# Seven block products in place of eight in one layer of a mixture-of-experts kernel, with its sums on VectorE and its row scatters respaced

## The chip, the core and the metric

The kernel runs on one core of a Trainium2 chip. TensorE (PE) multiplies, VectorE (DVE) and ScalarE (ACT) read its results from PSUM and work on SBUF, GpSimd (POOL) issues the indirect DMAs that scatter rows, and SyncE (SP) issues the other DMAs. [...]The metric is the device time of one execution in microseconds. Three runs of the kernel before took 1376.5, 1378.32 and 1379.24 us; the median is 1378.32.

## The reference

Two parts follow each other. The first takes the real part of a two-dimensional Fourier transform of each of 8 batches of 2496 rows and 256 columns. The second is a mixture of experts without dropped rows: each of the 19,968 rows goes to the one expert of eight that its logits choose, through two layers, and is scaled with its gate's probability.

```python
X = np.fft.fft(x, axis=1)
X = np.fft.fft(X, axis=2)
x = X.real.astype(np.float32).reshape(B * S, D)
...
logits = x @ w_gate
expert_idx = np.argmax(logits, axis=1)
...
for e in range(E):
    lo, hi = (boundaries[e], boundaries[e + 1])
    h = np.maximum(x_sorted[lo:hi] @ w1[e], 0.0)
    y_sorted[lo:hi] = h @ w2[e]
return (gate_w[:, None] * y).astype(np.float32)
```

Here D is 256, the hidden width F is 1024, and everything is float32.

## The kernel before

The work has two streams that are woven into one program by Python generators. The order of all instructions is written out by hand: each `yield` is a place where the other stream may put in its next piece.

**The side stream** makes rows out of a batch. `first` (L314) loads x, folds it on VectorE (L284 to L286, L295) and multiplies (tile s); its result passes through DRAM (`Td`, read back by `regroup`). `second` (L350) finishes the transform with the products p2 and p3 (both named p in the profile), copies on ScalarE (zz L368, zs L394, the mirrored rows L373) and the row sums on VectorE (lg L397, rows L399). `route` (L405) picks each row's expert and its place, ranks rows with small matmuls (rk), and scatters ten groups of 128 rows with indirect DMAs into the sorted store `Xs` in DRAM, one per yield. A batch is done in two halves, so it has 20 scatters. `close` then runs `plan` (L456), a chain of small VectorE instructions that turns the counts into a table of blocks: which rows of `Xs`, and which expert.

**The main stream** is `experts` (L530). It goes through 66 blocks in eight rounds; round b uses what batches 0 to b have put into `Xs`. Rounds 0 and 1 have blocks of 256 and 128 rows, round 2 has three blocks of 512 rows, rounds 3 to 7 have five of 512 rows each, and round 7 ends with 7 blocks of 256 and up to 21 of 128 rows. `fetch` (L504) loads a block's rows xb and its expert's w1 and w2 on SP's queue, one or two blocks ahead, three buffers each. `turn` (L517) transposes the rows of the next block on TensorE (tile pt) and VectorE writes them to xT. The first layer of a 512-row block has 8 chunks of 128 hidden columns; each chunk is a PSUM bank ph with two matmuls (the halves of D), and a Relu takes it to hT, by ScalarE (L584) for even chunks and VectorE (L582) for odd ones. The second layer has four output tiles py of 128 rows with eight matmuls each; ScalarE scales them into y (L598) and GpSimd scatters them to the output (L222). The transposes of the next block stand ahead of the first and second output tile.

**The weaving.** While round b-1 is worked on, batch b passes through `second` and batch b+1 through `first`; `mixed` (L632) is that side stream. Every chunk of the first layer counts one unit of work and every output tile two, 16 units a 512-row block. The main loop gives the side stream 44 ticks over 70% of a round's units:

```python
due += TICKS * w / (0.7 * total) if w else 1
while due >= 1:
    next(side, None)
    due -= 1
```

[...]three (`pm_`) for the side stream, two for ph, two for py and one for pt. All matmuls are recorded at L207 and all indirect DMAs at L222, since helpers issue them; they are told apart by their tiles.

Of the kernel before, what the change touches and what calls it, by code (L numbers as in the profile page):

```python
# [11 lines left out]
F32 = mybir.dt.float32  # L12
BF16 = mybir.dt.bfloat16
I32 = mybir.dt.int32
ALU = mybir.AluOpType
ACTF = mybir.ActivationFunctionType
AX_X = mybir.AxisListType.X
PSUM = bass.MemoryType.PSUM
# [162 lines left out]

TICKS = 44
WARM = 16
MOST = max(k for now in rounds() for _, k, _ in now)


# [15 lines left out]
def kernel(ctx: ExitStack, tc, x, w_gate, w1, w2, out):  # L202
# [39 lines left out]
    pm_ = ctx.enter_context(tc.tile_pool(name="pm_", bufs=3, space=PSUM))  # L242
    pst = ctx.enter_context(tc.tile_pool(name="pst", bufs=1, space=PSUM))
    psh = ctx.enter_context(tc.tile_pool(name="psh", bufs=2, space=PSUM))
    psy = ctx.enter_context(tc.tile_pool(name="psy", bufs=2, space=PSUM))

# [158 lines left out]
    def route(b, h, rows, lg):  # L405
# [40 lines left out]
        for s in range(NSL):  # L446
            sent(put_row(Xs, pi[:, s:s + 1], rows[:, s], E * CAP - 1, "xs"), b)
            yield

# [66 lines left out]

    def turn(size, xb):  # L517

        xT = bp.tile([128, 2, BIG], F32, tag="xT", name="xT", bufs=1)
        n = min(size // 128, 2)  # L520
        for h in range(-(-size // 256)):
            pt = pst.tile([128, 2, n, 128], F32, tag="t", name="pt")
            for c in range(2):
                for t in range(n):
                    nc.tensor.transpose(pt[:, c, t], xb[:, 2 * h + t, c * 128:(c + 1) * 128], ident[:])  # L525
            vec.tensor_scalar(xT[:, :, 256 * h:256 * h + 128 * n], pt[:].rearrange("p c t k -> p c (t k)"),  # L526
                              con["alt"][:], None, op0=ALU.mult)
            yield xT

    def experts(todo):  # L530

        got, xT, used = [], None, None

# [20 lines left out]
        for k, (b, size, last, at) in enumerate(todo):  # L556
            n, m = size // 128, BIG // size
            if not k:
                while todo[0][:3] not in tabs:
                    yield 0  # L560
                fetch_some(0)
                for _ in range(9):
                    yield 0
                for xT in turn(size, got[0][0]):
                    pass
# [6 lines left out]
            hT = bp.tile([128, FC, BIG], F32, tag="hT", name="hT", bufs=1)  # L572
            for f in range(FC // m):
                ph = psh.tile([128, m, size], F32, tag="h", name="ph")
                with needed(last, at, ph):
                    for j in range(m):
                        for c in range(2):
                            mm(ph[:, j], w1_sb[:, c, (m * f + j) * 128:(m * f + j + 1) * 128], xT[:, c, 0:size],
                               c == 0, c == 1)
                o = hT[:, m * f:m * (f + 1), 0:size]  # L580
                if f % 2:
                    vec.tensor_scalar(o, ph[:], 0.0, None, op0=ALU.max)  # L582
                else:
                    act.activation(o, ph[:], ACTF.Relu)  # L584
                yield 1
            if follow:
                while follow[:3] not in tabs:
                    yield 0
                fetch_some(k + 1, 2)
                turned = turn(follow[1], got[0][0])  # L590
            y = bp.tile([128, BIG // 128, D], F32, tag="y", name="y", bufs=3)
            for i in range(n):
                xT = next(turned, xT)
                py = psy.tile([128, D], F32, tag="y", name="py")
                with needed(last, at, py):
                    for f in range(FC):
                        mm(py[:], hT[:, f, i * 128:(i + 1) * 128], w2_sb[:, f], f == 0, f == FC - 1)
                act.activation(y[:, i], py[:], ACTF.Copy, scale=xb[:, i, D + 1:D + 2])  # L598
                put_row(out, ro[:, i:i + 1], y[:, i], NT - 1, "out")
                yield 2  # L600
            for xT in turned:
                pass

    def pads(b):
# [27 lines left out]
    def mixed(b):  # L632
# [5 lines left out]
        for k, _ in enumerate(two):  # L638
            if k % 2:
                next(one, None)  # L640
            yield
        yield from woven(close(b), one)

# [8 lines left out]
    nc.sync.dma_start(out=wg[:], in_=w_gate)  # L652
    for _ in range(WARM):
        pw = psy.tile([128, D], F32, tag="y", name="py")
        mm(pw[:], ones[:], bc(ones[:], 1, 2))
# [30 lines left out]
    for k, _ in enumerate(second(0)):  # L686
        if k % 2 == 0:
            next(early, None)
    work = experts(todo)
    for b in range(1, B):  # L690

        side, done, due = mixed(b), 0, 0.0
        if b == 1:
            side = woven(close(0), chain(early, side))
        total = 16 * sum(k * size for size, k, _ in rounds()[b - 1]) / BIG
        while done < total:
            w = next(work)
            done += w
            due += TICKS * w / (0.7 * total) if w else 1
            while due >= 1:  # L700
                next(side, None)
                due -= 1
        for _ in side:
            pass
    rest = pads(B - 1)
# [51 lines left out]
```

## Time and profile before

| | |
|---|---|
| median of three runs | 1378.32 us |
| profiled execution, its own time | 1381.33 us |
| span of its instructions | 1379.6 us |
| granted TensorE clock, mean over the span | 0.975 |
| ph, first layer (2016 matmuls, all block sizes) | 577.8 us busy |
| py, second layer (2560 matmuls) | 572.0 us busy |
| output scatters (163) on GpSimd | 159.1 us busy |
| row scatters (160) on GpSimd | 158.7 us busy |

A line of the groups reads: line, engine, operation, output tile, input tiles, shapes, count; then busy time and the mean length of one in ns; then the engine's idle time ahead of them and what ended most of it. A line of a timeline reads: start and length in us, engine, line, operation, tiles, count, and in brackets the idle time before it. The granted clock is below 1 in the first quarter of the span only: 0.73 from 0 to 100 us, 0.97 from 100 to 350 us, and 1.00 after that.

### The profile page before, as it was taken

The page shows a single profiled execution, that of the slowest core. Times are in us where ns is not written, and L with a number is a line of the kernel's source. Part 1 is how long each engine was busy: PE and PEld are TensorE (multiplying, and loading weights), DVE is VectorE, ACT ScalarE, POOL GpSimd, SP SyncE. Part 2 cuts the span into 40 slices and gives each one's busy share as a digit, 9 for nine tenths or more (in the row PEclk, how much of TensorE's full clock was granted, in tenths as well). Part 3 has the DMA queues.
Part 4 walks back from the last instruction along what each step waited for, and adds up shares of the span by engine and source line. Part 5 has one row for each costly group of instructions (what it writes and reads, how often), then busy time and mean ns, then how long its engine had stood idle before and what let it go on. Part 6 is the DMA issues. An engine that isn't in the chain of part 4 may idle for free.

```text
span 1379.6 us, 16917 instructions
## 1 busy us (share of the span) xinstructions
PE 1317.9 (96%) x6055; PEld 992.2 (72%) x6055; DVE 380.7 (28%) x1183; ACT 282.7 (20%) x656; POOL 325.8 (24%) x335
## 2 busy tenths in 40 slices
PE   5688898999999999999999999999999999999998
PEld 3567787676677677776677667776666779999887
DVE  4552244333232213332232221333211111111111
ACT  1322032221132112221132211221111111111111
POOL 0334224033122311324113311224131111111111
PEclk6779999999999999999999999999999999999999
DMA  8768756652555242553424342232452226777785
GB/s 252 244 240 297 284 191 218 260 177 83 234 177 177 82 176 103 192 184 129 157 85 139 142 174 92 107 119 78 162 190 93 88 87 240 264 273 273 257 316 199
DMA packets 63089, 249.50 MB, mean 181 GB/s; under 512 B 10057, under 2 KB 24883, under 8 KB 43420
## 3 DMA queue, kind: packets, MB, share of 16 engines
q1 hardware_dynamic: 46231, 203.33, 41.6%
q0 software_dynamic: 15888, 42.14, 8.4%
q10 hardware_dynamic: 885, 2.94, 0.6%
q8 instruction: 49, 0.80, 0.2%
q14 instruction: 36, 0.29, 0.1%
HBM read 194.97 MB, written 54.83 MB: 181 GB/s over the span
## 4 chain that ended last, share of the span: by engine, by line
PE 88%; issue 4%; DMA 3%; DVE 2%; another core or an unknown queue 1%; POOL 1%; ACT 1%; SPq 0%; POOLq 0%; ACTq 0%; DVEq 0%
PE py L207 39%; PE ph L207 38%; PE p L207 5%; PE s L207 3%; PE pt L525 3%; DMA xq<-in_x_dram 2%; POOL Xs L222 1%; DMA out_dram<-y,ro 1%; DMA Td<-t 0%; DVE hT L582 0%; DMA t<-Td 0%; DVE xq L295 0%; PE rk L207 0%; DMA xb<-Xs 0%
## 5 line engine op out<-in xcount | busy, mean ns | idle before, releaser
L207 PE MATMUL ph<-xT,w_sb 128*128 128x512 f32 (+2 forms) x2016 | 577.8, 440 | 11.2 <-ACT hT L584 2.6
L207 PE MATMUL py<-w_sb,hT 128*128 128x256 f32 x2560 | 572.0, 380 | 6.1 <-issue 6.1
L207 PEld LDWEIGHTS py<-w_sb,hT 128*128 128x128 f32 x2560 | 479.4, 190 | 67.8 <-issue 6.5
L207 PEld LDWEIGHTS ph<-xT,w_sb 128*128 128x128 f32 x2016 | 328.2, 192 | 209.8 <-issue 175.7
L222 POOL DMA_INDIRECT out_dram<-y,ro x163 | 159.1, 976 | 871.2 <-ACT y L598 848.4
L582 DVE TENSOR_SCALAR hT<-ph 128x512 f32<-128x512 f32 x163 | 112.7, 692 | 695.9 <-issue 330.6
L598 ACT ACTIVATE y<-py,xb 128x256 f32<-128x256 f32 x163 | 77.3, 474 | 606.0 <-PE py L207 525.4
L222 POOL DMA_INDIRECT Xs<-rows,pi x160 | 158.7, 992 | 177.0 <-issue 79.5
L584 ACT ACTIVATE hT<-ph 128x512 f32<-128x512 f32 x163 | 97.3, 597 | 320.7 <-PE ph L207 281.1
L526 DVE TENSOR_SCALAR xT<-pt,table 128x512 f32<-128x512 f32 (+1 forms) x94 | 63.4, 674 | 64.0 <-PE pt L525 62.5
L207 PE MATMUL s<-xq,w 104*112 104x256 f32 (+2 forms) x208 | 62.7, 426 | 12.2 <-DVE xq L286 11.1
L207 PEld LDWEIGHTS p<-table,t 120*128 120x128 f32 x352 | 55.0, 205 | 26.1 <-issue 19.4
L207 PE MATMUL p<-table,zz 128*128 128x145 f32 (+1 forms) x320 | 58.2, 308 | 9.3 <-ACT zz L368 4.6
L207 PE MATMUL p<-table,t 120*128 120x120 f32 (+1 forms) x352 | 58.2, 291 | 8.4 <-issue 5.2
L397 DVE COPY lg<-p 128x16 f32<-128x16 f32 x80 | 13.9, 174 | 189.4 <-ACT zs L394 164.5
L207 PEld LDWEIGHTS s<-xq,w 104*112 104x112 f32 x208 | 39.9, 207 | 25.8 <-DVE xq L286 9.8
L207 PEld LDWEIGHTS p<-table,zz 128*128 128x128 f32 x320 | 46.8, 199 | 14.2 <-issue 7.0
L525 PEld LDWEIGHTS pt<-table,xb 128*128 128x128 f32 x326 | 40.5, 142 | 17.6 <-issue 12.9
L525 PE MATMUL pt<-table,xb 128*128 128x128 f32 x326 | 51.7, 274 | 0.4 <-DMA xb<-Xs 0.4
L399 DVE SCALAR_TENSOR_TENSOR rows<-p,zs 128x129 f32<-128x129 f32 x160 | 48.3, 344 | 1.6 <-issue 0.6
L368 ACT COPY zz<-p 128x240 f32<-128x240 f32 (+1 forms) x88 | 31.1, 353 | 46.5 <-PE p L207 37.0
L310 ACT COPY t<-s 112x512 f32<-112x512 f32 x48 | 28.0, 584 | 54.8 <-PE s L207 44.6
(83 smaller groups left out, 305.6 us busy)
## 6 DMA issues: line engine op xcount, KB each, us to landing
w_sb<-in_moe_w_dram SPq DMA_DIRECT2D x132, 1024.0 KB
xq<-in_x_dram SPq DMA_DIRECT2D x24, 896.0 KB
xb<-Xs SPq DMA_DIRECT2D x28, 516.0 KB
Td<-t SPq DMA_DIRECT2D x18, 448.0 KB
t<-Td SPq DMA_DIRECT2D x8, 768.0 KB
t<-Td SPq DMA_DIRECT2D x8, 640.0 KB
xb<-Xs SPq DMA_DIRECT2D x13, 258.0 KB
xb<-Xs SPq DMA_DIRECT2D x25, 129.0 KB
```

The costliest lines, as they stand in the source:

```text
L207: nc.tensor.matmul(o, lhsT=lhsT, rhs=rhs, start=start, stop=stop, **kw)
L222: return unordered(pool.indirect_dma_start(out=dst, out_offset=bass.IndirectOffsetOnAxis(ap=idx, axis=0), in_=rows, in_offset=None, bounds ...
L310: act.copy(t1[:, 2 * half:2 * half + 2], ps[:])
L368: act.copy(zz[:, :, g * GP:g * GP + n], p2[:])
L397: vec.tensor_copy(lg[:, k:k + 2], p3[:, NY:NY + 2 * E].rearrange("p (m e) -> p m e", m=2))
L399: vec.scalar_tensor_tensor(rows[:, k + m, 0:NY], p3[:, 0:NY], zs[:, 0:1], zs[:, 1:], op0=ALU.add, op1=op)
L525: nc.tensor.transpose(pt[:, c, t], xb[:, 2 * h + t, c * 128:(c + 1) * 128], ident[:])
L526: vec.tensor_scalar(xT[:, :, 256 * h:256 * h + 128 * n], pt[:].rearrange("p c t k -> p c (t k)"), con["alt"][:], None, op0=ALU.mult)
L582: vec.tensor_scalar(o, ph[:], 0.0, None, op0=ALU.max)
L584: act.activation(o, ph[:], ACTF.Relu)
L598: act.activation(y[:, i], py[:], ACTF.Copy, scale=xb[:, i, D + 1:D + 2])
```

## The change

In rounds 3 to 7 the first layer of each 512-row block, the product of rows (512 x 256) with w1 (256 x 1024), is cut into two by two by two blocks and made from seven block products in place of eight, in Winograd's form of Strassen's scheme.

- `turn` adds, at its end, four differences of the halves of xT on VectorE (256 columns each, `right`).
- `Left` makes four sums and differences of quarters of w1 (512 columns each, two written over or beside w1 in `ws`). They are issued one at a time by `step`, two in each group of the preceding block's first layer.
- `seven` takes the place of the loop over chunks: two groups, each with seven products of 2 chunks x 256 rows in five PSUM banks a to e. Two products add onto a bank that still holds another (a and c). ScalarE copies the first product (p1), VectorE forms u2, u3 and three hidden quarters from PSUM, ScalarE applies the Relu.
- PSUM: the two ph, two py and one pt banks become the five banks a to e; blocks of the old kind use a and c for ph, b and d for py, e for pt.
- The output tile y becomes a tile for each 128 rows, with six buffers.
- A group of row scatters is put on a list (`waiting`), and `send` issues one: with every tick before batch 4; from batch 4 on, one for each 1.2 units of work, also within `seven`.
- No side work is woven into `seven` (its yields are marked full). The side stream gets 32 ticks over 65% of the units outside `seven`; the second layer's tiles of these blocks yield twice, with one unit each.

```diff
-TICKS = 44
+TICKS = 32
+LATE = 4
+SHARE, ROOM = 0.65, 1.2
+def halved(b, size):
+    return size == 512 and b > 2
...
         for s in range(NSL):
-            sent(put_row(Xs, pi[:, s:s + 1], rows[:, s], E * CAP - 1, "xs"), b)
-            yield
+            waiting.append((b, pi[:, s:s + 1], rows[:, s]))
...
+    class Left:
+        def __init__(self, w1_sb):
+            ws = bp.tile([128, 3, F // 2], F32, tag="ws", name="ws", bufs=2)
+            o = [ws[:, k] for k in range(3)]
+            a11, a12, a21, a22 = (w1_sb[:, c, k * F // 2:(k + 1) * F // 2] for k in range(2) for c in range(2))
+            self.all = a11, a12, o[2], a22, o[0], o[1], a21
+            self.due = deque([(o[0], a21, a22, add), (o[1], o[0], a11, sub), (a21, a11, a21, sub),
+                              (o[2], a12, o[1], sub)])
...
+    def right(xs, b11, b12, b21, b22):
+        o = [xs[:, k] for k in range(3)]
+        vec.tensor_tensor(o[0], b12, b11, op=sub)
+        vec.tensor_tensor(o[1], b22, o[0], op=sub)
+        vec.tensor_tensor(b12, b22, b12, op=sub)
+        vec.tensor_tensor(o[2], b21, o[1], op=sub)
+        return b11, b21, b22, o[2], o[0], o[1], b12
...
+        def product(g, k, o, fresh=True):
+            for j in range(fp):
+                f = g * fp + j
+                mm(o[:, j], l[k][:, f * 128:(f + 1) * 128], r[k], fresh and not j, j == fp - 1, skip_group_check=True)
+        for g in range(half // fp):
+            a, b, c, d, e = (pse.tile([128, fp, th], F32, tag=k, name=k) for k in "abcde")
...
+            product(g, 0, a)
+            act.copy(p1[:], a[:])
+            yield
+            product(g, 5, b)
+            vec.tensor_tensor(u2[:], p1[:], b[:], op=add)
+            yield
+            product(g, 6, d)
+            vec.tensor_tensor(u3[:], u2[:], d[:], op=add)
+            yield
+            product(g, 4, c)
+            vec.tensor_tensor(h22, u3[:], c[:], op=add)
+            step()
+            yield
+            product(g, 1, a, False)
+            act.activation(h11, a[:], ACTF.Relu)
+            act.activation(h22, h22, ACTF.Relu)
+            yield
+            product(g, 3, e)
+            vec.tensor_tensor(h21, u3[:], e[:], op=add)
+            act.activation(h21, h21, ACTF.Relu)
+            yield
+            product(g, 2, c, False)
+            vec.tensor_tensor(h12, u2[:], c[:], op=add)
+            act.activation(h12, h12, ACTF.Relu)
+            step()
+            yield
...
+            more = None
+            if follow and got and halved(follow[0], follow[1]):
+                more = Left(got[0][1])
+            if halved(b, size):
+                for _ in seven(size, left.all, xT, hT, more.step if more else lambda: None):
+                    yield 0.5, True
...
-                y = bp.tile([128, BIG // 128, D], F32, tag="y", name="y", bufs=3)
+                y = bp.tile([128, D], F32, tag="y", name="y", bufs=6)
...
-        total = 16 * sum(k * size for size, k, _ in rounds()[b - 1]) / BIG
+        blocks = [(size, k * size / BIG, halved(b - 1, size)) for size, k, _ in rounds()[b - 1]]
+        total = sum(k * (15 if seven_ else 16) for _, k, seven_ in blocks)
+        open_ = sum(k * (8 if seven_ else 16) for _, k, seven_ in blocks)
         while done < total:
-            w = next(work)
+            w, full = next(work)
             done += w
-            due += TICKS * w / (0.7 * total) if w else 1
+            if not full:
+                due += TICKS * w / (SHARE * open_) if w else 1
             while due >= 1:
                 next(side, None)
                 due -= 1
+                if b < LATE or not w:
+                    send()
+            room = min(room + w, 2)
+            if b >= LATE and room >= ROOM:
+                send()
+                room -= ROOM
```

## The prediction

> **What bounds the kernel now.** I read the page first: shares of engines, then the chain that ended last.
>
> ```profile
> PE 1317.9 (96%) x6055; PEld 992.2 (72%) x6055; DVE 380.7 (28%) x1183; ACT 282.7 (20%) x656; POOL 325.8 (24%) x335
> ...
> PE 88%; issue 4%; DMA 3%; DVE 2%; another core or an unknown queue 1%; POOL 1%; ACT 1%; SPq 0%; POOLq 0%; ACTq 0%; DVEq 0%
> ```
>
> TensorE is busy for 96% of the span and holds 88% of the chain. Busy matmuls overlap (one lasts 380 ns, the next starts sooner), so I measure them by spacing. The timeline of PE alone, over one 512-row block of round 4 without side work and the start of the next, gives it:
>
> ```profile
> 653.47 13.90 PE L207 MATMUL ph<-xT,w_sb 128*128 128x512 f32 x32
> 667.20 0.60 PE L525 MATMUL pt<-table,xb 128*128 128x128 f32 x4
> 667.64 3.62 PE L207 MATMUL py<-w_sb,hT 128*128 128x256 f32 x16
> 671.09 0.60 PE L525 MATMUL pt<-table,xb 128*128 128x128 f32 x4
> 671.53 10.53 PE L207 MATMUL py<-w_sb,hT 128*128 128x256 f32 x48
> 681.89 10.46 PE L207 MATMUL ph<-xT,w_sb 128*128 128x512 f32 x24
> ```
>
> The reader sees two things. First, the code issues 16 first-layer matmuls for a block (8 chunks times 2 halves of D) and the trace has 32: **each f32 matmul runs as two**. Missing this halves the gain and makes VectorE look like the bound. Second, there are no holes. The spacing is (13.90-0.59)/31 = 0.429 us for 512 columns, with 0.59 the last one's own length, and (10.53-0.38)/47 = 0.216 us for 256 columns: nearly the same per column. The granted clock is 1.00 from 350 us on, and the table by stretches shows PE busy for 771.1 of the 775 us from 350 to 1125. So time taken off PE here comes off the span, if nothing else fills it.
>
> The groups by shape give the other durations:
>
> ```profile
> L582 DVE TENSOR_SCALAR hT<-ph 128x512 f32<-128x512 f32 x163 | 112.7, 692 | 695.9 <-issue 330.6 <-PE ph L207 303.1 <-remote 34.0
> L584 ACT ACTIVATE hT<-ph 128x512 f32<-128x512 f32 x163 | 97.3, 597 | 320.7 <-PE ph L207 281.1 <-issue 34.1 <-remote 4.0
> L399 DVE SCALAR_TENSOR_TENSOR rows<-p,zs 128x129 f32<-128x129 f32 x160 | 48.3, 344 | 1.6 <-issue 0.6
> L284 DVE TENSOR_TENSOR xq<-xq 104x508 f32<-104x508 f32 x24 | 16.3, 681 | 0.3
> L284 DVE TENSOR_TENSOR pm<-xq 104x127 f32<-104x127 f32 x8 | 2.3, 284 | 12.0 <-DMA xq<-in_x_dram 12.0
> ```
>
> **Products removed.** Rounds 3 to 7 have five 512-row blocks each, 25 in all. Before, a block's first layer is 32 x 0.429 = 13.74 us. After, it is 7 products x 4 chunks x 2 = 56 matmuls of 256 columns: 56 x 0.216 = 12.10 us. Gain 1.64 us a block, **41.1 us** in all. The doubled weight loads (190 ns each) stay under the 0.216 us spacing, as in the py stretch.
>
> **Sums added.** VectorE gets 10 sums from PSUM, 4 weight sums (512 wide) and 4 row sums (256 wide) a block and loses 4 evictions; ScalarE has 10 instructions for 4. A weight sum is the 508-column row, 0.68 us. A row sum lies between the rows of 127 and 508 columns: 0.42 us. A sum of PSUM and SBUF has no row of its width: from below 0.68 us (SBUF alone); L399 reads PSUM and takes 344 ns for 129 columns where L284 takes 284 for 127, so I add 0.06: 0.75 us. VectorE gains 7.5+2.7+1.7-2.8 = 9.1 us a block, 228 us in all, on an engine now at 28%. The question is whether the order makes PE wait.
>
> In the stage only products stand on PE; side work waits for the second layer. One product is 4 matmuls, 0.864 us, and its result is there 0.65+0.38 = 1.03 us after its start. ScalarE takes 0.60; a handover is 0.04 in the trace. First group, from the start of the stage: p1 copied 1.07-1.67; u2 waits for the second product, 1.93-2.68; u3 2.80-3.55; h22 3.66-4.41; weight sum to 5.0; h21 5.39-6.14; the seventh product wants c at 5.18 and h22 has read it by 4.41; h12 6.25-7.00, its Relu to 7.64. Second group from 6.05: its p1 copy stands behind that Relu on ScalarE, 7.64-8.24; u2 8.28-9.03, u3 9.07-9.82, h22 9.86-10.61 (needed at 11.23); h21 waits for its product, 11.44-12.19. The next transposes use bank e, which h21 reads: they start at 12.23, PE was ready at 12.10. So PE waits 0.13 us a block: **+3.3 us**. Behind them py reads its last hidden chunks only after six pairs of matmuls; they are there.
>
> Each of these needs has 0.6 to 0.8 us to spare, so a VectorE or ScalarE that enters late costs little. Some 12 stages follow second layers full of side work; a lag of 1.5 us would push h22 past 5.18 by 0.66: at most +8 us, at least 0; I take **+2**, since the last side evictions (0.27+0.17+0.60 us) end about when u2 starts.
>
> Row sums are issued at the third output tile and first needed two tiles (6.9 us) later; left sums a stage ahead. That adds a wait on the next block's w1 in VectorE's queue, in front of h21. In round 4 the plan ended at 645.3 and its loads were issued from 646.6, inside a second layer that ended at 653.5; after, the plan again stands in the fourth block's second layer, some 11 us before the first left sum. Cost 0.
>
> **Scatters against VectorE.** [...]The trace of the opening shows both orders:
>
> ```profile
> 65.52 1.21 DVE L295 TENSOR_TENSOR xq<-xq 104x1024 f32<-104x1024 f32 x1
> ...
> 65.80 1.78 POOL L222 DMA_INDIRECT Xs<-rows,pi  x1 [0.30 <-issue]
> ...
> 75.70 0.97 POOL L222 DMA_INDIRECT Xs<-rows,pi  x1 [0.30 <-issue]
> 75.79 0.68 DVE L284 TENSOR_TENSOR xq<-xq 104x508 f32<-104x508 f32 x1
> ```
>
> A scatter that starts under a sum is longer by 0.8; a sum that starts under a scatter keeps its 0.68. [...]By the row: 0 for VectorE, up to 0.7 us a scatter for GpSimd (24% busy). I take the row: 0.
>
> **Side work.** Its PE work is unchanged and stands in the second layers, about 1.2 ticks per 1.73 us of py. Before, a tick came per 2.2 us, but eight of 14 py turns in a round had two in a row; after, some six of 26 turns have two. Cost 0; rival 1 prices the rest. The block plan leaves the first layer, where its chain of small VectorE instructions held up an hT eviction:
>
> ```profile
> 636.95 1.98 PE L207 MATMUL ph<-xT,w_sb 128*128 128x512 f32 x4 [0.94 <-DVE p_nb L466]
> ```
>
> The windows at 470, 630, 790 and 940-960 us show PE idle for 3.8 us in all. In the second layer only the row transposes hang on VectorE, with 3.4 us to spare: **-3.8** (ends -3.8 and 0). Rounds 0 to 2 change only in pace and scatters. POOL sends batch 0 back to back (1.28 us apart) from 52.9 to 80.5, and still will. PE idles 19 us from 100 to 350; I put ±6 on that, taken as 0. Output tiles: six single tiles for three of four rows hold 20 us of work against a write of some 7 us; banks a to e give every other block the two buffers it had, but for py of 128-row blocks, which has a 3.6 us ph stage between two uses and a 0.47 us eviction: 0.
>
> **Sum.** -41.1+3.3+2-3.8 = -39.6. The profiled execution took 1381.3 (span 1379.6): 1341.7. It lies 3.0 above the median of the runs, 1378.3, so a median of **1339**.
>
> **Rivals.**
> 1. Side work, squeezed into the second layers, makes PE wait for the small evictions between ticks. For it: the double tick at 706.33 took 2.99 us where its matmuls fill 2.74, so 0.25 was lost. Against: that stretch is 100% busy elsewhere. If half of 35 ticks in each of four rounds lose 0.25: +17, 1356; if all: 1374. Chance 0.13.
> 2. VectorE bounds the stage. If a sum from PSUM and SBUF ran at two cycles per element (the 1.22 us of the 1024-column L295), nine sums, three weight sums and the copies before the last h21 take 1.9+9x1.26+3x0.64+0.6 = 15.8 us against 13.74: +2.0 a block where the forecast has -1.5, 50.5 in all, less the 3.8 of the plan: 1425, **slower**. It decides from about 0.99 us a sum. Against: pos<-rk,base from PSUM and SBUF (215 ns, 80 columns) is no longer than pos<-pos,oh from SBUF alone (246). Chance 0.06.
> 3. The stage fits but its gain is lost elsewhere (late w1 at round changes, a longer opening): within 0.2% of before. Chance 0.02.
>
> The forecast has 0.79, between 1326 (no wait for e, opening -6) and 1355 (all lags, opening +6). To leave out no more than 0.2, the range runs to 1358. About 0.2% is what a measurement tells from no change. Faster 0.92, same 0.02, slower 0.06.
>
> **What will show it.** 56 matmuls of 256 columns in a stage at 0.216 us; stages of 12.1 to 12.4 us between P0 and the transposes, and a pt wait of about 0.1 us on h21; sums from PSUM at 0.69 to 0.75 us; VectorE near 610 us busy; the PE gaps at the plan gone. It is wrong if PE idles over 1 us in a stage, or between ticks of the second layer.

## The result, and the profile after

| | before | after |
|---|---|---|
| median of four runs each, the first pair | 1377.41 us | 1364.72 us |
| ratio, 95% interval | | 0.991 [0.989, 0.993] |
| profiled execution, span | 1379.6 us | 1362.3 us |
| start of the first 512-row block of round 3 | 360.8 us | 367.4 us |
| its 25 blocks of rounds 3 to 7 | 778.1 us | 753.9 us |

The change makes the kernel faster, but by 13 us at the medians and 17 us between the profiled spans, where the forecast had 39.6. The last two rows, taken from TensorE's timelines, say where: the opening loses 6.6 us, and the 25 blocks gain 24.2.

The page of the kernel after, shares of engines and the chain:

```profile
PE 1284.0 (94%) x6655; PEld 1103.7 (81%) x6655; DVE 581.0 (43%) x1533; ACT 368.9 (27%) x806; POOL 326.1 (24%) x335
...
PE 87%; DVE 4%; DMA 3%; issue 3%; another core or an unknown queue 1%; ACT 1%; POOL 0%; SPq 0%; POOLq 0%; DVEq 0%; ACTq 0%
```

VectorE is 200 us busier and still at 43%. New in the chain are VectorE's 4% (2 before). The timeline of TensorE over a block of round 4 without side work and without row scatters in its stage:

```profile
652.05 1.03 PE L215 MATMUL a<-xT,w_sb 128*128 128x256 f32 x4
652.91 1.03 PE L215 MATMUL b<-xs,ws 128*128 128x256 f32 x4
...
663.27 1.03 PE L215 MATMUL c<-xT,ws 128*128 128x256 f32 x4
664.22 0.66 PE L567 MATMUL pt<-table,xb 128*128 128x128 f32 x4
...
678.97 1.03 PE L215 MATMUL a<-xT,w_sb 128*128 128x256 f32 x4
```

A product comes every 0.863 us, the stage from the first product to the transposes is 12.17 us, and the block 26.92, where the same block was 28.43 before (653.47 to 681.89): 1.51 less, as the forecast had it. The loss is in other stages. The groups by shape:

```profile
L215 PE MATMUL a<-xT,w_sb 128*128 128x256 f32 x400 | 103.3, 381 | 5.0 <-ACT p L597 4.3 <-issue 0.8
L567 PE MATMUL pt<-table,xb 128*128 128x128 f32 x326 | 53.3, 279 | 10.8 <-DMA xb<-Xs 9.9 <-DVE hT L614 0.4
L215 PE MATMUL c<-xT,ws 128*128 128x256 f32 x200 | 52.3, 384 | 7.2 <-DVE hT L606 7.2
L600 DVE TENSOR_TENSOR u<-p,b 128x512 f32<-128x512 f32 x50 | 34.4, 688 | 182.3 <-PE b L215 141.1 <-ACT p L597 31.1 <-PE d L215 5.5
L614 DVE TENSOR_TENSOR hT<-u,e 128x512 f32<-128x512 f32 x50 | 34.3, 686 | 25.3 <-PE e L215 17.3 <-PE c L215 7.7 <-remote 0.2
```

The sums are no dearer than a weight sum of 512 columns: 0.69 us both (0.685 to 0.686 for ws). But TensorE waits 7.2 us for h22 (L606) and 4.3 us for p1 (L597) in the products c and a, and 9.9 us for a block's rows ahead of pt. Measured stage by stage, 16 of the 25 stages are 12.16 to 12.18 us, and nine are not:

| round | long stages, us |
|---|---|
| 3 | 13.02, 14.82 |
| 4 | 13.74, 15.31 |
| 5 | 13.11, 15.35 |
| 6 | 13.81, 14.75 |
| 7 | 14.63 (the pads) |

Together they are 19.0 us too long, and they are exactly the stages in which GpSimd sends row scatters back to back: seven or eight in each of the nine, none in the other 16. The timeline of all engines in the worst one:

```profile
783.82 1.03 PE L215 MATMUL a<-xT,w_sb 128*128 128x256 f32 x4
783.87 0.97 POOL L230 DMA_INDIRECT Xs<-rows,pi  x1 [0.30 <-issue]
784.67 0.69 DVE L614 TENSOR_TENSOR hT<-u,e 128x512 f32<-128x512 f32 x1 [1.95 <-PE c L215]
...
785.15 0.97 POOL L230 DMA_INDIRECT Xs<-rows,pi  x1 [0.30 <-issue]
...
786.84 1.13 PE L215 MATMUL c<-xs,ws 128*128 128x256 f32 x4 [0.27 <-DVE hT L618]
788.98 0.58 ACT L597 COPY p<-a 128x512 f32<-128x512 f32 x1 [1.53 <-PE c L215]
...
789.62 0.70 PE L215 MATMUL a<-xT,w_sb 128*128 128x256 f32 x2 [1.65 <-ACT p L597]
```

Read the copy of p1 at 788.98. Its product a ended at 784.85, ScalarE was free from 787.45, and it starts 1.53 us after that, 4.1 us after the product's end. Likewise h21 (L614) reads bank e, whose product ended at 783.12, and starts 1.55 us later on an idle VectorE. In the quiet stage such handovers take 0.04 to 0.17 us. Handovers from VectorE and ScalarE stay short in the long stages too, at 0.03 to 0.06 us in 42 cases of 43. The trace's own record of TensorE's semaphore shows the same: four updates, of products that ended at 784.85, 785.71, 786.58 and 787.98, stand within 0.18 us at 788.91 to 789.08. **TensorE goes on issuing; its reports come late, and then all at once.** (I call the semaphore update that ends a wait on TensorE its report. The trace gives a product 1.03 us whether its report is late or not, as it does the a at 783.82, whose report stands at 788.91. So a late write to PSUM and a late semaphore can't be told apart here.)

### The profile page after: what moved, and what is told of

The parts are those of the page before. It is cut to its first block, busy times and chain, and to the rows that moved or that the text cites. A ratio compares the mean times of both kernels' runs of the same rounds, so it can differ in the third digit from the quotient of the medians.

```text
span 1362.3 us, 18852 instructions
## 1 busy us (share of the span) xinstructions
PE 1284.0 (94%) x6655; PEld 1103.7 (81%) x6655; DVE 581.0 (43%) x1533; ACT 368.9 (27%) x806; POOL 326.1 (24%) x335
## 3 DMA queue, kind: packets, MB, share of 16 engines
q0 software_dynamic: 15888, 42.14, 8.5%
## 4 chain that ended last, share of the span: by engine, by line
PE 87%; DVE 4%; DMA 3%; issue 3%; another core or an unknown queue 1%; ACT 1%; POOL 0%; SPq 0%; POOLq 0%; DVEq 0%; ACTq 0%
PE py L215 40%; PE ph L215 14%; PE a L215 6%; PE c L215 6%; PE p L215 6%; PE b L215 3%; PE d L215 3%; PE pt L567 3%; PE s L215 3%; PE e L215 3%; DMA xq<-in_x_dram 1%; DMA Td<-t 1%; DMA xb<-Xs 1%; DVE hT L606 0%
## 5 line engine op out<-in xcount | busy, mean ns | idle before, releaser
L215 PE MATMUL py<-w_sb,hT 128*128 128x256 f32 x2560 | 580.2, 381 | 6.3 <-DVE hT L682 4.0
L215 PE MATMUL ph<-xT,w_sb 128*128 128x128 f32 (+2 forms) x1216 | 221.2, 337 | 8.7 <-issue 4.1
L215 PEld LDWEIGHTS ph<-xT,w_sb 128*128 128x128 f32 x1216 | 178.0, 192 | 40.4 <-issue 19.7
L682 DVE TENSOR_SCALAR hT<-ph 128x512 f32<-128x512 f32 x63 | 43.5, 691 | 298.5 <-issue 204.1
L600 DVE TENSOR_TENSOR u<-p,b 128x512 f32<-128x512 f32 x50 | 34.4, 688 | 182.3 <-PE b L215 141.1
L215 PE MATMUL a<-xT,w_sb 128*128 128x256 f32 x400 | 103.3, 381 | 5.0 <-ACT p L597 4.3
L215 PEld LDWEIGHTS a<-xT,w_sb 128*128 128x128 f32 x400 | 75.4, 190 | 17.3 <-ACT p L597 5.5
L684 ACT ACTIVATE hT<-ph 128x512 f32<-128x512 f32 x63 | 37.6, 597 | 114.2 <-PE ph L215 78.8
L610 ACT ACTIVATE hT<-a 128x512 f32<-128x512 f32 x50 | 29.9, 597 | 137.2 <-PE a L215 117.0
L215 PE MATMUL c<-xT,ws 128*128 128x256 f32 x200 | 52.3, 384 | 7.2 <-DVE hT L606 7.2
```

The source lines that it names most:

```text
L215: nc.tensor.matmul(o, lhsT=lhsT, rhs=rhs, start=start, stop=stop, **kw)
L600: vec.tensor_tensor(u2[:], p1[:], b[:], op=add)
L610: act.activation(h11, a[:], ACTF.Relu)
```

## The experiments

The theory after this comparison: **trains** of back-to-back scatters on GpSimd make TensorE's reports late, and the tight stage can't take it. Rivals: **load** (VectorE's own sums make the stage too tight), **overlap** (a weight sum and a scatter at the same time hold each other up; in the opening a scatter under a sum took 1.78 us for 0.97), **presence** (any scatter in the stage does it, spaced or not). For the opening: the block tables are ready later.

### Scatters out of the stage, sums out of the stage, more ticks, pacing

Sends in the second layers alone:

```diff
-SHARE, ROOM = 0.65, 1.2
+SHARE, ROOM = 0.65, 0.8
-            room = min(room + w, 2)
-            if b >= LATE and room >= ROOM:
+            if not full:
+                room = min(room + w, 2)
+            if b >= LATE and not full and room >= ROOM:
```

> The kernel after with no row scatter in the first layers of the seven products: they are sent in the second layers alone, 1.25 for each unit of work there. Burst theory (while GpSimd issues row scatters back to back, TensorE's results reach VectorE and ScalarE 0.8 to 1.5 us late, and the tight stage cannot take it): the eight long stages of rounds 3 to 6 (13.0 to 15.3 us) go back to 12.2, the stage with the pads (14.6) stays, so 16 us less than after, 1349; if trains of scatters spill over from the second layer into the stage, part of it remains, 1349 to 1358. Load theory (VectorE's own sums make the stage too tight, whatever GpSimd does): no change, 1365.[...]

Weight sums at the end of the second layer:

```diff
-                for _ in seven(size, left.all, xT, hT, more.step if more else lambda: None):
+                for _ in seven(size, left.all, xT, hT, lambda: None):
```

> The kernel after with the four weight sums of a block taken out of the first layer and issued at the end of the second one. Burst theory: VectorE in the stage is lighter by 2.7 us, but what is late is TensorE's report, so the long stages stay within 1 us of what they were: 1358 to 1366. Load theory[...]: the long stages go back to 12.2 us, 1346; the first products that use a sum may then wait at the head of a stage, at most 25 x 0.7 = 17 us against it, seen as idle ahead of b or c.

More ticks ahead of batch 4:

```diff
-                due += TICKS * w / (SHARE * open_) if w else 1
+                due += (40 if b < LATE else TICKS) * w / (SHARE * open_) if w else 1
```

> The kernel after with 40 ticks in place of 32 in the rounds before batch 4 alone. If the opening loses its 6.6 us since the block tables of the next round are ready later than before (345.6 for 340.8 us), TensorE's two waits for the first block's rows at the round changes (6.60 and 3.30 us) shrink to under 2 us each and the time falls by 6 to 10, 1355 to 1359. If the rows are late for another reason, the waits stay and the time is 1365. The stages of seven products stay as they are in both.

Pacing (`mark` holds one number of the tile that the stage wrote last):

```diff
             if b >= LATE and room >= ROOM:
+                if full and waiting:
+                    pool.tensor_copy(dot[:], mark[0])
                 send()
```

> The kernel after with each row scatter inside a stage of seven products made to wait for a result of that stage (GpSimd first copies one number of the tile that was written last), so that the scatters really stand about 2.1 us apart. Burst theory: as many scatters in the stage, but no train of them: the long stages fall to 12.2 to 12.7 us, 1348 to 1354. Rival, presence theory (each scatter in the stage delays a report, back to back or not): long stages stay above 13 us, 1360 to 1366. Load theory: no change, 1365.

| | time | ratio to before (1355.49) |
|---|---|---|
| scatters outside | 1376.40 | 1.015 [1.013, 1.017] |
| sums outside | 1337.97 | 0.987 [0.984, 0.990] |
| 40 early ticks | 1315.56 | 0.970 [0.969, 0.972] |
| paced | 1329.49 | 0.981 [0.980, 0.983] |

Before took 1355.5 here, 22 us less than in the first pair, and no stage was long because of a train in any of the four, not even with the scatters left as they are (40 ticks: all 25 stages at 12.16 to 12.17, with the same trains 1.28 us apart). So these four say nothing on trains yet. They do settle three things.

**Load and overlap fall**: the sums and the trains stand in the same stages as in after, and the stages are 12.17. Taking the sums out only costs: the second product waits for them (0.73 us in six stages, 1.60 in two, 0.56 in one). The row of the timeline, sums outside:

```profile
845.46 1.13 PE L215 MATMUL b<-xs,ws 128*128 128x256 f32 x4 [1.60 <-DVE ws L546]
```

**Scatters outside was a miss**: the stages are 12.17, but the 20 scatters of a batch then take longer, so the next round's table is ready at 493.7 us where after, undisturbed, has it at 466.5 (a run told below), and at each of four round changes TensorE waits some 9.6 to 10.0 us for rows:

```profile
499.01 1.09 PE L567 MATMUL pt<-table,xb 128*128 128x128 f32 x4 [9.61 <-DMA xb<-Xs]
```

**The opening is settled.** TensorE's timeline of the kernel after at the changes to rounds 2 and 3:

```profile
245.50 1.11 PE L567 MATMUL pt<-table,xb 128*128 128x128 f32 x4 [6.60 <-DMA xb<-Xs]
...
350.93 0.66 PE L567 MATMUL pt<-table,xb 128*128 128x128 f32 x4 [3.30 <-DMA xb<-Xs]
```

and with 40 early ticks, the same two places:

```profile
227.84 0.60 PE L567 MATMUL pt<-table,xb 128*128 128x128 f32 x4
...
323.78 0.60 PE L567 MATMUL pt<-table,xb 128*128 128x128 f32 x4
```

Both waits are gone. The table of round 3 is ready at 304.4 us, where after undisturbed has 327.5.

### Both kernels again, trains doubled, both remedies

> The kernel after, unchanged, beside the kernel before, once more. In the four experiments so far the kernel before took 1355.5 us where the compared pair has 1377, and no stage of seven products was long, in the one with the row scatters left as they are (the one with 40 ticks) either. If the late reports under trains of scatters belong to the chip or the moment of the first pair and not to the change, after has no long stage here, and takes 1329 to 1332 (the paced experiment, 1329.5, differs from it by the pacing alone): a ratio of 0.980 to 0.983. If the long stages are there again, 1345 to 1348, 0.993, and the pacing is what removed them.

> The kernel before, unchanged, for its trace. If late reports are what made it slower in the first pair, its gaps of TensorE on an eviction to hT at 470, 630, 790 and 940 to 960 us (3.8 us in all) are gone here, though the block plan still stands in the first layer; if the block plan made them, they are still there. Most of the 22 us by which it is faster here should lie ahead of 350 us, where reports are waited for at once (tiles p, s, rk): 15 or more of the 22.

Pacing and 40 early ticks together:

> The kernel after with 40 ticks before batch 4 and with the paced scatters. Where reports are prompt the pacing has nothing to gain: 1315 to 1317, as with 40 ticks alone. Where they are late: 1330 to 1335, and no stage over 12.7 us.

Each scatter from batch 4 on twice:

```diff
             sent(put_row(Xs, idx, rows, E * CAP - 1, "xs"), b)
+            if b >= LATE:
+                put_row(Xd, idx, rows, E * CAP - 1, "xd")
```

> The kernel after with each row scatter from batch 4 on issued twice, the second time to a store that nothing reads: trains of scatters twice as long, 12 and more in a stage. If trains make reports late on every chip and only their length decides, stages of seven products between 13 and 17 us appear again. If the lateness is not the trains' own, all stages stay at 12.2; what is then longer are the waits for xb at the round changes, since a block's rows land later (as in the experiment with the scatters outside): up to 10 us each at five changes.

| | time | ratio to before (1388.10) |
|---|---|---|
| after | 1373.92 | 0.989 [0.986, 0.992] |
| before, one run | 1389.18 | |
| both remedies | 1349.84 | 0.971 [0.969, 0.974] |
| doubled, one run | 1521.80 | |

Now reports were late again, for every kernel: after's nine stages are 13.78 to 15.56 us. Doubled trains make the eight stages of rounds 3 to 6 30.8 to 34.9 us long; the others stay at 12.17, and the pads' stage (not doubled) at 14.70. That is about twice the 13 to 17 us that was forecast. **So the length of the trains decides, where reports are late at all.** With pacing the eight are 12.2 to 13.2 us, where 12.7 at most was forecast; the pads, not paced, made 16.6. This version is 34 us slower than the one with 40 ticks and prompt reports, and its stages are only 8.3 us of that: its round 3 starts at 365.6 us where the other's starts at 338.5. The opening of after, too, ends later where reports are late (367.4 and 370.2 us against 350.3 with prompt ones). Which waits of the opening make this was not taken apart.

The single run of before was late as well, so its trace could not show what was asked of it. It has TensorE's gaps on hT at three of the four places (2.3 of 3.8 us) and none at the second, with the same instructions in the same order.

The condition is the chip's at the time, not the kernel's: the same program runs with prompt or with late reports (after took 1364.72 and 1373.92 us with late ones, and 1329.41 with prompt ones in a set told below), and keeps the one or the other through a whole set of runs, as far as the times tell. It marks the trace as well. Of the same program, 954 updates of TensorE's semaphore are recorded where reports are late and 1014 where they are prompt, and in the pages the time to landing of DMAs is missing in the first and there in the second. One line of the DMA issues of after, late and prompt:

```profile
xb<-Xs SPq DMA_DIRECT2D x28, 516.0 KB
```

```profile
xb<-Xs SPq DMA_DIRECT2D x28, 516.0 KB, 3.6
```

What makes the condition stays open. The record names chip 11 for this late set and for the next one, which is prompt. It is not the profiling: the runs of after without it took 1370 to 1377, the profiled one 1375.7.

### What it is in a train, and spacing everything

The second scatter with all indices out of bounds, or a plain DMA of the same rows in its place:

```diff
-                put_row(Xd, idx, rows, E * CAP - 1, "xd")
+                put_row(Xd, nowhere[:, 0:1], rows, E * CAP - 1, "xd")
```

```diff
-                put_row(Xd, idx, rows, E * CAP - 1, "xd")
+                at.append(128 * len(at))
+                nc.sync.dma_start(out=Xd[at[-1]:at[-1] + 128], in_=rows)
```

> As the kernel with every row scatter from batch 4 on issued twice, but the second one has all its indices out of bounds, so that it writes nothing: GpSimd issues as many instructions, TensorE's reports meet only half of the written rows. If it is GpSimd's issuing [...]that holds TensorE's reports up, the long stages are as long as with both scatters written, 31 to 35 us. If it is the writing of rows, they are as long as in the kernel after, 13.8 to 15.6 us. On a chip with prompt reports every stage is 12.2 and nothing is told.

> As the kernel with every row scatter from batch 4 on issued twice, but the second one is a plain DMA of the same 128 rows of 1032 bytes on SyncE's queue, to a store that nothing reads: the same bytes in the same pieces, without GpSimd. If the moved bytes hold TensorE's reports up: 20 to 35 us in the long stages. If GpSimd's issuing does: 13.8 to 15.6 us as in the kernel after.

In the first the software queue moved 42.2 MB, as in after, where the doubled kernel moved 52.5: nothing is written out of bounds. The packets of that queue are as many as in the doubled kernel, though: 19,728 in both, and 15,888 in after. They took 1338.53 and 1327.94 us beside 1356.97 for before: reports were prompt, and nothing is told. Nor is it by the next two kernels, which had four such cases each in one program (1330.45 and 1338.89 beside 1355.56). In the second of these one stage of 20.5 us shows another thing: GpSimd had so much to send that the last output scatters and with them the loads of w1 came late, and the left sum in VectorE's queue, which waits for w1 (VectorE idles 8.83 us for it), held up h21 and h12 behind it, and TensorE for 6.3 us.

> One kernel, four cases side by side, one for each batch: batch 4's row scatters as in the kernel after; batch 5's each issued twice, the second to a store that nothing reads; batch 6's with a second one whose indices are all out of bounds, so that it writes nothing; batch 7's with a plain DMA of the same 128 rows on SyncE's queue as the second. Where reports are late, the two long stages were 13.8 and 15.6 us for plain and 32 to 34 us for doubled scatters. If GpSimd's issuing holds TensorE's reports up: batch 6 like batch 5, batch 7 like batch 4. If the written rows do: batch 6 like batch 4, and batch 7 over 20 us. If it is the indirect writes of GpSimd's queue alone: 6 and 7 both like batch 4. If batch 4's stages are 12.2, the chip has prompt reports at the time and nothing is told.

> A second kernel of four cases: batch 4's row scatters doubled as before; batch 5's with a second scatter of one number (4 bytes) a row in place of 258; batch 6's with two copies of 128x256 on GpSimd in place of a second scatter, so that GpSimd is busy but issues nothing; batch 7's with the second one out of bounds. Where reports are late: batch 4 has stages of 32 us. If GpSimd's issuing[...] holds reports up, batch 5 is like batch 4 (over 25 us), batch 7 too, batch 6 at most 17. If the moved bytes do, batch 5 is under 17. If a busy GpSimd does, batch 6 is over 20. Where reports are prompt all stages are 12.2.

A third program with four cases ran twice, prompt (1326.12 beside 1356.94) and then late (1428.15 beside 1373.80).

```diff
+            if b == 4:
+                put_row(Xd, idx, rows, E * CAP - 1, "xd")
+            if b == 5:
+                put_row(Xd, nowhere[:, 0:1], rows, E * CAP - 1, "xd")
+            if b == 6:
+                for _ in range(2):
+                    pool.tensor_copy(pad[:, 0:D], pad[:, 0:D])
+            if b == 7:
+                at.append(128 * len(at))
+                nc.sync.dma_start(out=Xd[at[-1]:at[-1] + 128], in_=rows)
```

> One kernel, four cases: beside each row scatter of batch 4 a second one to a store that nothing reads; of batch 5 a second one with all indices out of bounds; of batch 6 two copies of 128x256 on GpSimd (0.9 us together), so that it is busy but issues nothing; of batch 7 a plain DMA of the same rows on SyncE's queue. The control is the stage with the eight pads, 14.6 to 15.1 us where reports are late. If GpSimd's issuing holds TensorE's reports up: over 28 us with batch 4 and 5, under 17 with 6 and 7. If the written rows do: over 28 with batch 4 alone. If a busy GpSimd does: over 20 with batch 6. If moved bytes do: over 20 with batch 7. If the pads' stage is 12.2, reports are prompt and nothing is told.

> The kernel with four cases once more, since reports were prompt the first time: the readings are those stated before. If GpSimd's issuing holds TensorE's reports up: over 28 us with batch 4 (doubled) and 5 (out of bounds), under 17 with 6 (busy GpSimd) and 7 (plain DMA). If the written rows do: over 28 with batch 4 alone. If a busy GpSimd does: over 20 with batch 6. If moved bytes do: over 20 with batch 7. If the pads' stage is 12.2, reports are prompt and nothing is told.

| beside each row scatter | its two stages, prompt | late |
|---|---|---|
| a second scatter, written | 12.16, 12.17 | 28.48, 31.74 |
| a second one, out of bounds | 12.17, 12.16 | 31.53, 31.26 |
| 0.9 us of copies on GpSimd | 12.17, 12.17 | 12.17, 12.17 |
| a plain DMA of the rows | 12.17, 12.17 | 12.17, 16.34 |
| the pads (control) | 12.16 | 14.48 |

A scatter that writes no row holds the reports up as much as one that does. A plain DMA of the same rows adds nothing clear to the train that stands in these two stages anyway: 12.17 and 16.34 lie below and above the 13.0 to 15.6 us of after. A busy GpSimd does no harm between spaced scatters (12.17). **What harms is indirect DMAs issued by GpSimd back to back, whatever they write.** Two things stay open: a scatter out of bounds sends as many packets as a written one, so GpSimd's issuing and the packets of its queue are not told apart; and these late figures are of one run. The late run's timeline of TensorE, first a stage with out-of-bounds scatters, then one with copies:

```profile
630.23 1.03 PE L215 MATMUL e<-xs,w_sb 128*128 128x256 f32 x4
642.72 2.08 PE L215 MATMUL c<-xT,ws 128*128 128x256 f32 x4 [11.46 <-DVE hT L620]
646.85 2.07 PE L215 MATMUL a<-xT,w_sb 128*128 128x256 f32 x4 [2.05 <-ACT hT L624]
...
847.53 1.03 PE L215 MATMUL e<-xs,w_sb 128*128 128x256 f32 x4
848.39 1.03 PE L215 MATMUL c<-xT,ws 128*128 128x256 f32 x4
```

and GpSimd's in the same two stages:

```profile
639.13 0.98 POOL L231 DMA_INDIRECT Xs<-rows,pi  x1 [0.30 <-issue]
640.41 0.97 POOL L231 DMA_INDIRECT Xd<-rows,nowhere  x1 [0.30 <-issue]
...
847.83 1.17 POOL L231 DMA_INDIRECT Xs<-rows,pi  x1 [0.31 <-issue]
848.99 0.88 POOL L472 COPY pad<-pad 128x256 f32<-128x256 f32 x2
850.22 1.39 POOL L231 DMA_INDIRECT Xs<-rows,pi  x1 [0.35 <-issue]
```

In the first, scatters start 1.28 us apart, and the next product waits 11.46 us for an h22 whose own product had ended at 628.03. In the second they start 2.2 us apart on average (844.3 to 855.3, six of them), and nothing waits: the copies space the scatters. So spacing is a remedy, shown here for 2.2 us and nearly so in the paced kernel (2.1 us meant; 0 to 1.1 us left a stage). So the presence rival falls: scatters in the stage do no harm as such.

What after is worth with prompt reports, and the trace of before once more:

> The kernel after, unchanged, a second time. If the kernel before takes about 1356, reports are prompt, all stages of seven products are 12.2, and after takes 1328 to 1332, a ratio of 0.979 to 0.983. If before takes 1377 to 1390, reports are late, and the ratio is 0.989 to 0.991 as in the two earlier pairs.

> The kernel before, unchanged, for its trace where reports are prompt (1356). Its gaps of TensorE on hT at about 470, 630, 790 and 940 to 960 us (3.8 us in all) are gone, though the block plan still stands in the first layer, if late reports made them; they are still there if the plan made them. Its first 512-row block of round 3 starts at 339 to 344 us, some 8 to 12 us ahead of that of the kernel after (about 350): what the change loses in the opening. If reports are late: 1377 to 1390, with the gaps.

After took 1329.41 beside 1356.94 for before: 0.979 [0.976, 0.982], and each of its 25 stages is 12.16 or 12.17. Before's single run (1373.44) fell at a time of late reports, so its opening with prompt reports has no trace. The forecast for that case was that the gaps would be there, and they are gone all the same. TensorE's timeline of that run at the end of the stage in which, in the first trace, ph waited 0.94 us for the plan's VectorE instructions:

```profile
630.45 3.60 PE L207 MATMUL ph<-xT,w_sb 128*128 128x512 f32 x8
633.88 0.60 PE L525 MATMUL pt<-table,xb 128*128 128x128 f32 x4
```

and VectorE's, with the plan in the same stage:

```profile
631.26 0.14 DVE L466 TENSOR_TENSOR p_nb<-base,p_gone 1x8 f32<-1x8 f32 x1
```

The plan runs there without a gap, so the plan alone does not make one. All 25 blocks of this run have the bare 772.3 us, 5.8 less than in the first trace, and the 5.8 lie at the four places of the gaps. It also limits the theory: as in the first trace, 13 indirect DMAs in a row stand ahead of each of these places (one of the trains: 773.3 to 788.6 us), and TensorE waits at none. So at a late time not every train makes reports late. If this run's blocks and what follows them are as long as in a prompt run, its 17 us more lie ahead of the blocks.

Spacing everything: each row scatter from the opening on waits for the newest result of the main stream, the pads go out over the second layers of two blocks, and fewer scatters are sent for a unit of work; first with 40 ticks in all rounds, then with 32 from batch 4 on.

```diff
-SHARE, ROOM = 0.65, 1.2
+SHARE, ROOM = 0.65, 1.3
+            if mark:
+                pool.tensor_copy(dot[:], mark.pop())
             b, idx, rows = waiting.popleft()
...
-    for _ in work:
-        next(rest, None)
+    for k, (_, full) in enumerate(work):
+        if not full and k % 2:
+            next(rest, None)
```

> A better version by the burst theory: 40 ticks in every round, one row scatter for each 1.5 units of work from batch 4 on (was 1.2), each made to wait for the newest result of the main stream, in the opening too, and the pads spread over two blocks' second layers. Burst theory, on a chip with late reports: all stages of seven products at 12.2 to 12.6 us where the version with 40 early ticks and pacing in the stage alone had up to 13.2, and 16.6 with the pads: another 7 us of the stages, and up to 8 of the opening: 1335 to 1345 where the kernel before takes 1388, 0.962 to 0.969. If late reports need only a scatter and no train, no better than that version, 0.971. On a chip with prompt reports: 0.970, as with 40 ticks alone (1315 for 1355).

> The spaced version with 32 ticks again from batch 4 on (40 ahead of it), one row scatter for each 1.3 units, each waiting for the newest result of the main stream, pads spread. With prompt reports the stages of 13.4 to 13.5 us that 40 ticks left in three rounds (3.2 us) go back to 12.2: 1317, 0.970 of the kernel before. With late reports: all stages within 0.5 us of 12.2, and a ratio of 0.960 to 0.967.

They took 1320.76 beside 1356.97, 0.974 [0.972, 0.976], and 1315.07 beside 1355.56, 0.969 [0.968, 0.971]. With 40 ticks throughout, VectorE's side work runs into the second stage of rounds 3 to 5 (13.4 to 13.5 us); with 32 all stages are 12.2. Reports were prompt both times: that these two hold up where reports are late was not measured. There the paced version with 40 early ticks is the best measured: 0.971.

## Why the prediction was wrong, point by point

| step of the prediction | forecast | first pair | prompt reports |
|---|---|---|---|
| products, and pt waiting for e | -41.1 + 3.3 = -37.8 | -37.4 | -37.4 |
| late entry into the stage | +2 | +19.0 | 0 |
| the plan leaving the stage | -3.8 | -5.8 (for another reason: see below) | 0 |
| rounds 0 to 2 | 0, at most ±6 | +6.6 | about +8 |
| sum | -39.6 | -17.3 | -27.5 |

The first pair's column lacks 0.3 us that after loses behind the 25 blocks. The -37.4 is the 25 blocks of after with prompt reports (734.9) against the 772.3 of before's last run; 25 times the 1.51 of the quiet block gives 37.8. The -5.8 is what before lost at its four gaps in the first pair (778.1 less 772.3), and what after is rid of. "About +8" is an estimate, as before has no trace with prompt reports: its median 1356.9 less 1.7 for what lies outside the span, 240.7 for the rest after the 25 blocks and 772.3 leaves a start of round 3 at 342.2, where after has 350.3. That column's rows sum to -29; some 2 us of the rest are in the blocks after round 7's 512-row ones. By the same estimate late reports had cost both kernels much the same ahead of round 3 in the first pair (360.8 for 342.2, and 367.4 for 350.3), so that loss hardly shows in the comparison.

- **Right**: two hardware matmuls for each f32 one (a product's two are four in the trace), 0.863 us a product, stages of 12.17 us with a pt wait of 0.1, sums at 0.69, VectorE at 581 us busy (about 610 forecast), the second layers unchanged (14.75 us of the quiet block), and w1 in time for the left sums. Rival 2 (VectorE as the bound) and rival 1 (squeezed side work, 17 to 35 us) did not happen.
- **"Scatters against VectorE ... I take the row: 0"** failed. The row tells what a scatter does to a VectorE instruction's length, and there 0 was right: 0.684 to 0.688 us in every group. The harm came by another way, the report from TensorE, which no row of lengths shows: 19.0 us in the first pair. The trace of before had it: ScalarE and VectorE idle for 4.6 to 4.9 us ahead of hT evictions at 795 and 797 us, at the end of a train, where they idle for 2.7 to 2.8 ahead of the evictions before (the lines stand below).
- **"The block plan leaves the first layer: -3.8"** failed, and is the same error from the other side. The row named p_nb as what ended the wait; it was only the VectorE instruction ahead of the late eviction. The gap was counted as a gain of moving the plan, instead of as a sign that trains make TensorE's reports late, which the tighter stage would feel more. In the first pair the gaps did cost before 5.8 us, so the row's number came near by luck.
- **"Each of these needs has 0.6 to 0.8 us to spare ... I take +2"** was mis-sized: the bound of 8 us assumed one lag of 1.5 us at the head of a stage. The lag comes in the middle and again and again while the train lasts, 0.9 to 3.2 us a stage. Before, two ph banks gave 1.7 us of slack and lost 5.8 us over the 25 blocks; the chain of sums lost 19.0. The prediction's own sign of being wrong was there: TensorE idle for over 1 us in a stage (1.65 at 789.62).
- **"Rounds 0 to 2 change only in pace and scatters ... ±6, taken as 0"** failed in sign and slightly in size. Pace was the point: 32 ticks over 65% of a round, with `while waiting` taking ticks too, end the side stream later than 44 over 70%, and the next round's first block waited 6.60 and 3.30 us for its rows. 40 ticks take both waits away and, ratio against ratio (0.970 and 0.979 with prompt reports), 0.9% of the time, 12 us; the two waits were 7.6 us of it (4.37 and 3.26 in after's prompt run), and what the rest is was not told apart. All of the 12 us lie ahead of round 3 (338.5 us for 350.3).

The lines of before behind the second point, two evictions in time and two late ones of one stage:

```profile
789.48 0.60 ACT L584 ACTIVATE hT<-ph 128x512 f32<-128x512 f32 x1 [2.78 <-issue]
791.20 0.69 DVE L582 TENSOR_SCALAR hT<-ph 128x512 f32<-128x512 f32 x1 [2.74 <-issue]
...
794.65 0.60 ACT L584 ACTIVATE hT<-ph 128x512 f32<-128x512 f32 x1 [4.57 <-PE ph L207]
796.78 0.69 DVE L582 TENSOR_SCALAR hT<-ph 128x512 f32<-128x512 f32 x1 [4.89 <-remote]
```

So rival 3 ("its gain is lost elsewhere") came true in part: more than half of the gain where reports are late, under a third where they are prompt.

## What to carry to other kernels

A stage whose chain hands a result to another engine every 0.9 us has the slack of its shortest need, and late reports (here by 1.5 to 4.1 us) eat it. Look in the trace of before at handovers (the start of the reader less the end of the producer), not at lengths of instructions, and see under what they grow. An instruction that a profile names as ending a wait may only be the neighbour of the late one: check whether it, too, started late before a gain is booked on moving it. Work that is spaced in program order is not spaced in time on an engine that waits for nothing (1.28 us between scatters where 2.1 were meant); to space it, give it something of the other stream to wait for.

## What the runs showed of the hardware that was not expected

- At some times GpSimd's indirect DMAs, issued 1.28 us apart, hold TensorE's reports up by 1 to 4 us once some six to eight have gone out in a row (with breaks of no more than 0.6 us), and by over 10 us in a train more than twice as long (TensorE waits 11.46 us for one in the late run with four cases). TensorE itself goes on issuing, its matmuls 0.216 us apart under a train (777.78 to 784.68 in the first trace of after); the news of their results comes late. With prompt reports the same trains do nothing (25 stages of 12.16 or 12.17 us), and in one late run of before they did nothing either.
- The same before-kernel took 1355 to 1357 us (medians) with prompt reports and 1373 to 1388 (medians, and a single run at the low end) with late ones.
- After a long wait TensorE ran slower for a while. Table by stretches of the late run with four cases, columns busy time and count of PE, PEld, DVE, ACT, POOL, then granted clock, DMA share and GB/s:

```profile
636.00:648.00 12.00, 3.23 (x7) 2.15 (x8) 3.06 (x5) 1.48 (x3) 6.29 (x7) 0.50 0.11 35
648.00:657.00 9.00, 9.00 (x34) 7.25 (x33) 5.10 (x9) 3.42 (x7) 0.00 (x0) 0.74 0.00 1
```

The granted clock is 0.50 in the stretch with the 11.46 us wait, and the products after it start 1.7 to 1.9 us apart in place of 0.86: a part of the long stages of the doubled trains is this (the four gaps from 646.85 to 653.26 add 3.0 us to a stage of 31.53). In the opening of after in the first pair the clock is 0.51 from 351.5 to 355.0, behind the wait of 3.30 us. Its waits in the stages, 1.73 us at most, do not show it: the granted clock is 1.00 from 380 to 1130 us. In its second late run waits of 2.10 and 2.54 us in a stage did, and in the late run with four cases one of 1.66 us (the two products behind it start 1.84 and 1.67 us apart): each has 3.4 us at 0.50 close behind it. So not every wait of some 1.7 us did it.
